# Neighborhood attention on one core: the start regrouped (mark copies, fills, first shifts and PSUM banks moved between engines)

## The chip, the cores and the metric

The kernel runs on 1 core of one Trainium2 chip. The metric is device time in microseconds (us) of one execution; the profile adds one profiled execution with every instruction's engine, start and duration. Engines: PE does matrix products, DVE, ACT and POOL do elementwise work and copies, and SP only issues transfers (DMA). Each engine takes its instructions in order; an engine's queue of DMA issues is named SPq, ACTq or POOLq here. Matrix products land in PSUM, which has eight banks; everything else lies in SBUF, 128 partitions wide.

## The reference

The input is a 224 x 224 image with 192 channels in bf16. Every pixel attends to the 7 x 7 pixels around it with a step of 2, the window clamped at the borders, with one softmax over the 49:

```
qkv = x @ wqkv;  q, k, v = split(qkv)
r0 = clip(ir - 6, 0, H - 13);  ri = r0[:, None] + 2 * arange(7)     # the same for columns
logits = einsum('bnc,bnkc->bnk', q, k[neighbours]) * 192 ** -0.5
p = softmax(logits)
o = einsum('bnk,bnkc->bnc', p, v[neighbours]) @ wo
```

## The kernel before

**Folded weights.** Logits are x_q (Wq Wk^T) x_k, so the kernel forms AW = Wq Wk^T (scaled) once and then G = AW applied to the queries; the keys are x itself. In the same way WP = Wv Wo is formed once, and V = x WP already has the output projection in it.

**Layout.** Because the step is 2, pixels of odd and even rows and columns don't mix; rows are kept in two classes `rc`, columns in two classes `cc`. `load_items(b)` (line 145) brings in one strip `b` of 16 image rows by three transposing DMAs on SP, so that channels lie on partitions: XA[0] and XA[1] hold 128 channels each of the even and the odd pixel of a column pair, and X1[b] the 64 that are left of both. `xb_items` (158) copies the latter into XB[0] and XB[1], 64 partitions each. The other 64 partitions of XB hold marks: rows of numbers that, multiplied with a one-hot row or column of G, add a very negative value to the logits of keys outside of the window. `marks(m, v0, v1, eng)` (227) copies a block of rows of such marks; XB has 48 rows of each class, used as a ring. `sort_items(b, rc, eng)` (167) and `first_sort` (365) copy a strip into XS in the order in which V is computed.

**Steps and pairs.** The work goes in 14 steps `n`: seven tiles `ti` of 16 class rows, for each of the two row classes. A step has 14 column slots `s`, taken two at a time in seven pairs `m`. A pair goes through:

- stage1: logits `s` on PE (line 497), their negated maximum `nmx` on DVE (499)
- stage1b: the exponentials `p` on ACT (507)
- stage2, one pair later: transposes of `p` on PE (517), copied to SBUF by DVE (519)
- stage3, two pairs later: P V on PE (528) with V from VF and VD
- stage4: the reciprocal of the sums (534) and the product (548) on DVE, then the store (554, 567), mostly on SP, a part on POOL through a list `pool_q`, of which four entries are issued in a pair.

**V and its shifts.** `v_item(rc, cb)` (343) computes V of one column slot into a PSUM tile `pv` and has DVE or ACT evacuate it into VF. VD is VF with the two halves of the partitions exchanged, made by DMAs: `vd_low` (350) and `vd_high` (354). For step 0, V of the rows above comes from `v_first` (358), seven products evacuated by ACT, and the first shifts (line 621) write it into the low half of VD[0] by two DMAs of 64 x 7 pieces.

**G.** For each step four groups of column slots are made: `whole(0)`, `whole(1)` and `halves` (437 to 456). A whole goes from PSUM into G by one evacuation; halves go over `gx`, which ACT evacuates and POOL then copies into G (456). The first group of step 0 is put directly, by ACT and DVE. G's own one-hot rows and columns for the marks are filled by `g_col` (248) and `g_row` (258); `g_row_on` (274) copies such rows on to further slots by DMA.

**Interleaving.** While step n runs its pairs, PE also computes V and G for step n + 1. In step 0 these are its own remaining V (list `v0`) and G as well, in the lists `w128` (677) and `w64` (657). The argument given to an item says whether DVE (true) or ACT evacuates it. The PSUM pools are `ps_g` (three banks, for G and V), `ps_o` (two, for P V), `ps_t` (one) and two for the logits.

**Order.** All queues are written out by hand: the order of the statements is the order on each engine, and `in_order` (89) fixes it. Before the loop (lines 593 to 621) stand the fills of G, the third strip's loads, the sorts and copies of strips 0 and 1, the second block of marks (243 and 604), `v_first`, a warming-up of PE (610) and the first group of G.

Of the kernel before, what the change touches and what calls it, by code (L numbers as in the profile page):

```python
# [9 lines left out]
F32 = mybir.dt.float32  # L10
# [16 lines left out]
MM = 16  # L27
BND = 16 * S
C = 192
VP = 2 * C + 2  # L30
# [68 lines left out]
def kernel(  # L99
# [7 lines left out]
    nc = tc.nc  # L107
# [37 lines left out]
    def load_items(b):  # L145

        src = xp[16 * b:16 * b + 16].rearrange("r j c -> (r j) c")
        at = (16 * b) % (2 * RP) * S

        def one(k):  # L150
            if k == 1:
                X1[b] = x1_p.tile([128, BND], BF, name=f"x1_{b}", tag="x1")
            dst = X1[b][:] if k == 1 else XA[k // 2][:, at:at + BND]
            nc.sync.dma_start_transpose(out=dst.unsqueeze(1), in_=src[:, 128 * k:128 * k + 128])

        return [lambda k=k: one(k) for k in ((0, 2, 1) if b in (0, 2, 3) else (1, 0, 2))]
# [70 lines left out]
    def marks(m, v0, v1, eng):  # L227

        p = 64 - XDAT[m]
        if v0 == 0:  # L230
            eng(out=_win(XB[m], p, 64, S, [[RW, MM], [1, S]]), in_=_win(XB[m], p, 64, 0, [[RW, MM], [1, S]]))
        else:
            eng(out=_win(XB[m], p, 64, v0 * RW, [[1, (v1 - v0) * RW]]), in_=_win(XB[m], p, 64, v0 % MM * RW, [[1, (v1 - v0) * RW]]))
# [6 lines left out]

    for m in range(2):
        marks(m, 0, MM, nc.vector.tensor_copy)
    marks(0, MM, 2 * MM, nc.vector.tensor_copy)

# [1 line left out]
    def g_col(rc, ti, s0, ns, eng):  # L248
        for cc in range(2):
            p = XCOL[cc]  # L250
            if s0 == 0:
                for h in range(2):
                    for (j0, nj) in _runs8(rc, ti, h):
                        eng(out=_win(G[rc][cc], p, 32, NSLOT * 128 + 64 * h + 8 * j0, [[nj, 8], [1, nj]]), in_=_win(CH[cc], p, 32, 0, [[1, 8], [0, nj]]))
            else:
                eng(out=_win(G[rc][cc], p, 32, (NSLOT + s0) * 128, [[128, ns], [8, 16], [1, 8]]), in_=_win(CH[cc], p, 32, 8 * s0, [[8, ns], [0, 16], [1, 8]]))

    def g_row(rc, ti, s0, ns, eng, parts):

        for cc in range(2):  # L260
            p = XROW[cc]
            for (j0, nj, e0, estep) in parts:
                if s0 == 0:
                    for h in range(2):
                        for (r0, nr) in _runs8(rc, ti, h):
                            a, b = max(j0, 8 * h + r0), min(j0 + nj, 8 * h + r0 + nr)
                            if a < b:
                                eng(out=_win(G[rc][cc], p, 32, NSLOT * 128 + 64 * h + 8 * r0 + a - 8 * h - r0, [[nr, 8], [1, b - a]]),
                                    in_=_win(E, p, 32, e0 + estep * (a - j0), [[0, 8], [estep, b - a]]))
                else:  # L270
                    eng(out=_win(G[rc][cc], p, 32, (NSLOT + s0) * 128 + 8 * j0, [[128, ns], [8, nj], [1, 8]]),
                        in_=_win(E, p, 32, e0, [[0, ns], [estep, nj], [0, 8]]))
# [68 lines left out]
                    nc.tensor.matmul(pv[64 * h:64 * h + 64, cc * C:(cc + 1) * C], lhsT=at(k, h), rhs=WP[(cc, pas)][:], start=(pas == 0), stop=(pas == 1))  # L341

    def v_item(rc, cb):
        def emit(dve):
            pv = ps_g.tile([128, 512], F32, name="pv", tag="pg")
            v_mms(pv, lambda k, h: XS[rc][:, k, cb, 64 * h:64 * h + 64])
            evac(_win(VF[rc], 0, 128, cb * VP, [[193, 2], [1, C]]), pv[:, 0:2 * C].rearrange("p (t c) -> p t c", c=C), dve)
        return emit

    def vd_low(rc, c0, c1, eng=nc.sync):  # L350

        eng.dma_start(out=VD[rc][0:64, c0:c1, 0:VP - 1], in_=VF[rc][64:128, c0:c1, 0:VP - 1])
# [240 lines left out]
    g_row(0, 0, 0, 1, pool, first0)  # L593
    g_col(0, 0, 1, 3, pool)
    g_row(0, 0, 1, 3, pool, first0)
    g_col(0, 0, 4, 10, pool)
    g_col(1, 0, 0, 1, pool)
    g_row(1, 0, 0, 1, pool, first1)
    g_row(1, 0, 1, 1, pool, first1)
    for it in load_items(2):  # L600
        it()
    for it in first_sort(dve) + xb_items(0, dve) + xb_items(1, dve) + sort_items(0, 0, dve):
        it()
    marks(1, MM, 2 * MM, dve)
    for j in range(7):
        v_first(j)(False)

# [7 lines left out]
    gw0[0](False)  # L615
    gw0[1](True)
    gh0[0](False, True)
    g_row_on(0, 4, 10)

    for (c0, c1) in ((7, 14), (0, 7)):  # L620
        nc.scalar.dma_start(out=VD[0][0:64, c0:c1, 0:VP - 1], in_=VF[1][0:64, 7:14, 0:VP - 1])
    v0 = [v_item(0, cb) for cb in (13, 0, 1, 2, 3, 4, 5, 6, 7, 8, 9, 10, 11, 12)]
    ld = []

    for k in range(NP + 2):
        J = pairs[k] if k < NP else None
        n = J.n if J else NSTEP
        w64, w128 = [], []
        if J:
            m = J.m  # L630
            if m == 0 and n + 1 < NSTEP:
                rc1 = steps[n + 1][1]
                gw, gh = g_all(n + 1)
                vs = [v_item(rc1, cb) for cb in range(NSLOT)]
            if n == 0:
                w128 = (v0[:9] + gw0[2:4], v0[9:] + gw0[4:6], gw0[6:8] + vs[0:3], gw[0:2] + vs[3:6], gw[2:4] + vs[6:9], gw[4:6] + vs[9:12], gw[6:8] + vs[12:])[m]
                w64 = (gh0 + gh)[m + 1:m + 2]
            elif n + 1 < NSTEP:
                w128 = gw[m + (m > 1):m + 1 + (m > 0)] + vs[2 * m:2 * m + 2]
                w64 = gh[m // 2:m // 2 + 1] if m % 2 == 0 else []  # L640
            stage1(J, 0)
            stage1(J, 1)
            stage1b(J, 0)
            if m == 0 and n + 3 < NBAND:
                ld = load_items(n + 3)
        if k == NP:
            stage2(pairs[k - 1])
        if k >= 2:
            stage3(pairs[k - 2], 0)
            stage3(pairs[k - 2], 1)  # L650
            if k >= NP:
                stage4a(pairs[k - 2], 0)
                stage4a(pairs[k - 2], 1)
            stage4(pairs[k - 2], 0)
            if k == NP - 1:
                stage4a(pairs[k - 2], 1)
        for it in w64:
            it(False)
        if J:
            stage1b(J, 1)  # L660
        if 1 <= k < NP:
            stage2(pairs[k - 1])
        if k >= 2:
            stage4(pairs[k - 2], 1)
        if not J:
            continue

        if m == 1 and 0 < n and n + 1 < NSTEP:
            vd_low(rc1, 9 if n == 1 else 7, 14)
        if n == 0 and m in (4, 6):  # L670
            vd_low(0, *((0, 5) if m == 4 else (5, 9)), nc.scalar)
        if 0 < n and m == 5 and n + 2 < NSTEP:
            vd_low(J.rc, 0, 7)
        if ld:
            ld.pop(0)()
        for i, it in enumerate(w128):
            it(n == 0 and i % (2 if m < 3 else 3) == 1)
            if n == 0 and it is v0[6]:
                vd_high(0, 13, 14)
                vd_high(0, 0, 6)  # L680
            if n == 0 and it is v0[13]:
                vd_high(0, 6, 13)
            if it is vs[6]:
                vd_high(rc1, 0, 7)
            if it is vs[13]:
                vd_high(rc1, 7, 14)
        if n == 0 and m == 0:
            for q in range(2):
                marks(q, 2 * MM, 2 * MM + 3, pool)
        if n == 0 and m == 1:  # L690
            first_vd()
            g_row_on(1, 2, 12)
            g_col_on()
            for it in xb_items(2, dve):
                it()
        if n == 0 and m >= 3:
            marks_on(m % 2, 2 * MM + 3 + (m - 3) // 2)
        add = []
        if n == 0:
            add = {0: sort_items(1, 1, pool), 1: sort_items(2, 1, pool), 3: sort_items(2, 0, pool), 5: xb_items(3, pool) + sort_items(3, 0, pool)}.get(m, [])  # L700
        else:
            if m == 0 and n + 2 < NBAND:
                add = sort_items(n + 2, J.rc, pool)

            if m in (2, 4) and n + 3 < NBAND:
                srt = sort_items(n + 3, J.rc, pool)
                one, two = xb_items(n + 3, pool) + srt[2:], srt[:2]
                add = (two if m == 4 else one) if n > 1 else one + two if m == 4 else []
        pool_q[:0] = add
        if n == 1 and m == 1:  # L710
            g_col(0, 1, 0, 1, pool)
            g_row(0, 1, 0, 1, pool, ((0, 16, MM - 6, 1),))
            g_row(0, 1, 1, 13, pool, ((0, 6, MM - 6, 1),))
        if n == 12 and m == 1:
            last = ((0, 9, 0, 1), (9, 7, 9, 0))
            g_col(1, 6, 0, 1, pool)
            g_row(1, 6, 0, 1, pool, last)
            g_row(1, 6, 1, 13, pool, last[1:])
        pool_do(4 if n + 1 < NSTEP else 3)
# [34 lines left out]
```

## Time and profile before

| What | us |
| --- | --- |
| median of 3 runs (lowest to highest) | 363.57 (362.75 to 363.65) |
| the profiled execution: its time | 363.5 |
| its span | 361.7 |
| busy: PE | 333.8 (92%) |
| DVE | 314.1 (87%) |
| ACT | 307.8 (85%) |
| POOL | 284.4 (79%) |

The busy shares are means over the whole span. In the first three slices of the page, 9 us each, PE is busy for 4, 7 and 7 tenths, ACT for 6, 4 and 4, DVE for 8, 9 and 5 and POOL for 8, 9 and 6; from the eighth slice on PE shows 9 in most. A line of the chain or of the timeline reads: start, length, engine, line of the kernel, what is written from what, number of instructions, and in brackets the idle time before it and what ended it. A group reads: line, engine, operation, count, then busy time in us and mean length of one in ns, then idle time. An engine's length of a DMA issue is the time that its queue was held, not that of the transfer.

### The profile page before, as it was taken

How to read it: one execution, taken by the hardware profiler on the slowest of the kernel's cores; microseconds unless marked ns; L12 is line 12 of the kernel's file. 1: busy time of each engine (PE TensorE's matmuls, PEld its weight loads, DVE VectorE, ACT ScalarE, POOL GpSimd, SP SyncE). 2: the span in 40 equal slices, each digit the busy share in tenths (PEclk: the TensorE clock that was granted, in tenths of full speed). 3: DMA queues.
4: the chain of work that ended last, by engine and by line, in shares of the span. 5: the costliest groups of instructions: out<-in, count | busy, mean ns of one | idle time of the engine just before them, and what ended most of it. 6: DMA issues, size and time to landing. Idle time of an engine off the chain costs nothing.

```text
span 361.7 us, 19481 instructions
## 1 busy us (share of the span) xinstructions
PE 333.8 (92%) x8120; PEld 307.4 (85%) x8120; DVE 314.1 (87%) x743; ACT 307.8 (85%) x824; POOL 284.4 (79%) x450
## 2 busy tenths in 40 slices
PE   4778888998999999999999999999999999999881
PEld 2667777997999999999989999998999999999671
DVE  8956987897898998989989899898998889989992
ACT  6445676897999999989999999998999989999792
POOL 8966699999896996959969699695995868374094
PEclk9989999999999999999999999999999999999998
DMA  9999886699979979889798997988989965634432
GB/s 189 208 184 166 176 167 159 153 178 180 208 155 208 195 166 175 192 192 197 169 188 188 178 193 179 181 202 179 194 186 187 176 144 122 141 96 110 105 78 77
DMA packets 137746, 60.79 MB, mean 168 GB/s; under 512 B 88809, under 2 KB 137134, under 8 KB 137659
## 3 DMA queue, kind: packets, MB, share of 16 engines
q1 hardware_dynamic: 130133, 56.37, 78.7%
q0 software_dynamic: 5520, 1.73, 2.7%
q10 hardware_dynamic: 2006, 1.47, 2.1%
q8 instruction: 63, 1.03, 1.2%
q14 instruction: 24, 0.20, 0.2%
HBM read 0.29 MB, written 19.27 MB: 54 GB/s over the span
## 4 chain that ended last, share of the span: by engine, by line
PE 71%; POOL 10%; DVE 9%; ACT 4%; DMA 2%; issue 2%; POOLq 0%; SPq 0%; DVEq 0%; ACTq 0%
PE pv L341 17%; PE s L497 15%; PE o_ps L528 14%; PE pg L421 10%; PE pt_ps L517 9%; PE pgh L421 5%; POOL out_dram L567 4%; ACT p L507 3%; POOL xs L170 2%; DVE xb L160 2%; POOL out_dram L554 2%; DMA vd<-vf 1%; DVE nmx L499 1%; POOL xb L160 1%; POOL g L456 1%
## 5 line engine op out<-in xcount | busy, mean ns | idle before, releaser
L507 ACT ACTIVATE p<-s,nmx 128x224 bf16<-128x224 f32 x392 | 149.7, 449 | 26.7 <-DVE nmx L499 24.9
L499 DVE TENSOR_REDUCE nmx<-s 128x2 f32<-128x392 f32 (+1 forms) x196 | 102.5, 565 | 19.1 <-PE s L497 17.8
L456 POOL COPY g<-gx 64x512 bf16<-64x512 bf16 (+1 forms) x110 | 61.8, 562 | 56.1 <-ACT gx L331 49.0
L548 DVE TENSOR_TENSOR o_sb<-o_ps,rs 128x384 bf16<-128x384 f32 x179 | 99.8, 557 | 6.2
L341 PE MATMUL pv<-wp,xs 128*64 128x192 bf16 x1624 | 93.2, 251 | 11.4 <-DVE xs L366 3.5
L341 PEld LDWEIGHTS <-xs 128*64 128x64 bf16 x1624 | 79.4, 112 | 24.7 <-issue 9.3
L331 ACT CAST vf<-pv 128x384 bf16<-128x384 f32 x193 | 87.4, 520 | 12.4 <-PE pv L341 11.7
L567 POOL DMA_DIRECT2D out_dram<-o_s x150 | 84.2, 568 | 1.1 <-issue 1.1
L497 PE MATMUL s<-xa,g 128*64 128x196 bf16 (+6 forms) x990 | 82.7, 233 | 2.0 <-DVE g L329 1.1
L528 PE MATMUL o_ps<-vd,pt_sb 128*64 128x193 bf16 x784 | 81.8, 246 | 2.4 <-ACT pt_sb L519 2.1
L497 PE MATMUL s<-xb,g 128*64 128x196 bf16 (+6 forms) x990 | 82.2, 232 | 0.6 <-DVE g L329 0.4
L528 PE MATMUL o_ps<-vf,pt_sb 128*64 128x193 bf16 x784 | 81.9, 247 | 0.1
L497 PEld LDWEIGHTS <-g 128*64 128x64 bf16 x1980 | 78.0, 110 | 4.5 <-issue 2.0
L528 PEld LDWEIGHTS <-pt_sb 128*64 128x64 bf16 x1568 | 71.5, 109 | 4.0 <-ACT pt_sb L519 3.1
L519 DVE COPY pt_sb<-pt_ps 128x1024 bf16<-128x1024 bf16 x93 | 63.7, 686 | 6.1 <-PE pt_ps L517 1.1
L517 PE MATMUL pt_ps<-ident,p 128*64 128x128 bf16 x1568 | 64.2, 219 | 0.0
L517 PEld LDWEIGHTS <-p 128*64 128x64 bf16 x1568 | 57.5, 110 | 5.0
L331 ACT CAST g<-pg 128x512 bf16<-128x512 f32 (+4 forms) x136 | 57.6, 468 | 2.2 <-PE pg L421 2.0
L421 PEld LDWEIGHTS <-aw 128*64 128x64 bf16 x1320 | 55.1, 110 | 3.8 <-issue 0.8
L421 PE MATMUL pg<-xb,aw 128*64 128x512 bf16 (+9 forms) x440 | 54.5, 269 | 0.1
L421 PE MATMUL pg<-xa,aw 128*64 128x512 bf16 (+9 forms) x440 | 52.5, 270 | 0.3 <-DMA xa<-in_x_dram 0.3
L170 POOL COPY xs<-xa 128x896 bf16<-128x896 bf16 x50 | 45.1, 928 | 1.4
(68 smaller groups left out, 277.7 us busy)
## 6 DMA issues: line engine op xcount, KB each, us to landing
vd<-vf SPq DMA_DIRECT2D x49, 336.9 KB
out_dram<-o_sb SPq DMA_DIRECT2D x156, 96.0 KB
out_dram<-o_sb SPq DMA_DIRECT2D x26, 78.0 KB
out_dram<-o_s POOLq DMA_DIRECT2D x78, 9.0 KB, 3.8
vd<-vf SPq DMA_DIRECT2D x2, 337.8 KB
vd<-vf ACTq DMA_DIRECT2D x2, 336.9 KB
xa<-in_x_dram SPq DMA_TRANSPOSE x28
out_dram<-o_s POOLq DMA_DIRECT2D x26, 15.0 KB, 3.8
```

What stands on the lines that cost most here:

```text
L331: nc.scalar.copy(out=out_, in_=in_)
L341: nc.tensor.matmul(pv[64 * h:64 * h + 64, cc * C:(cc + 1) * C], lhsT=at(k, h), rhs=WP[(cc, pas)][:], start=(pas == 0), stop=(pas == 1))
L421: nc.tensor.matmul(o, lhsT=l, rhs=r, start=(pas == 0), stop=(pas == 1))
L456: nc.gpsimd.tensor_copy(out=G[rc][cc][p:p + 64, 1, s0:s0 + ns, :], in_=gx[p:p + 64, 0:ns * 128].rearrange("p (s q) -> p s q", q=128))
L497: nc.tensor.matmul(o, lhsT=w, rhs=r, start=(pas == 0), stop=(pas == 1))
L499: nc.vector.tensor_reduce(out=nmx[:], in_=_win(s_ps, 0, 128, lo, [[256, 2], [16, 14], [1, 16 - lo]]), axis=AX.XY, op=ALU.max, negate=True)
L507: nc.scalar.activation(out=J.p[:, ab, cc, :, z:z + 112].rearrange("p q (r k) -> p q r k", k=8), in_=_win(s_ps, 0, 128, cc * 256, [[8, 2], ...
L517: nc.tensor.transpose(pt_ps[64 * h:64 * h + 64, 4 * ab + 2 * cc + q, :], J.p[:, ab, cc, q, 64 * h:64 * h + 64], ident[:])
L519: (nc.scalar.copy if J.n == NSTEP - 1 and J.m < 5 else nc.vector.tensor_copy)(out=J.pt[:], in_=pt_ps[:])
L528: nc.tensor.matmul(o_ps[64 * h:64 * h + 64, cc * 193:cc * 193 + 193], lhsT=J.pt[:, 4 * ab + 2 * cc + q, 64 * h:64 * h + 64], rhs=V[h][:, ( ...
L548: nc.vector.tensor_tensor(out=o_sb[:], in0=_win(o_ps, 0, 128, 0, [[194, 2], [1, C]]), in1=rs[:].unsqueeze(2).to_broadcast([128, 2, C]), op ...
L567: pool_q.append(lambda dst=dst, p=p, m=n * nj, cc=cc: nc.gpsimd.dma_start(out=dst.rearrange("j i c -> i j c"), in_=o_sb[p:p + m, cc, :]))
```

## The change

It touches the start and step 0 only; the computation is the same.

- The second block of marks (rows 16 to 31) is copied by POOL for both XB tiles: the first after the first shifts and a sort, the second at the end of pair 0. Before, DVE did both, at lines 243 and 604.
- The fills `g_col(0, 0, 4, 10)`, `g_col(1, 0, 0, 1)` and `g_row(1, 0, 0, 1)` go from POOL to ACT.
- `g_row_on(0, 4, 10)`, two DMAs on SP, moves ahead of the loads of strip 2.
- The first shifts are issued on POOL's queue instead of ACT's; the sort of strip 1 for class 1 follows them on POOL, ahead of the loop instead of behind pair 0.
- In pairs 0 and 1, four and two of the V products use `ps_o`'s banks, and DVE evacuates six of 11 items and four of seven, where it evacuated five and three.
- The two low shifts of pairs 4 and 6 go from ACT's queue to SP's.
- In step 0 a load of a later strip is issued behind the items of `w128` and their shifts, not ahead of them.

```diff
-    marks(0, MM, 2 * MM, nc.vector.tensor_copy)
...
     def v_item(rc, cb):
-        def emit(dve):
-            pv = ps_g.tile([128, 512], F32, name="pv", tag="pg")
+        def emit(dve, spare=False):
+            pv = ps_o.tile([128, 512], F32, name="pv", tag="o") if spare else ps_g.tile([128, 512], F32, name="pv", tag="pg")
...
-    g_col(0, 0, 4, 10, pool)
-    g_col(1, 0, 0, 1, pool)
-    g_row(1, 0, 0, 1, pool, first1)
     g_row(1, 0, 1, 1, pool, first1)
+    g_col(0, 0, 4, 10, act)
+    g_col(1, 0, 0, 1, act)
+    g_row(1, 0, 0, 1, act, first1)
+    g_row_on(0, 4, 10)
     for it in load_items(2):
         it()
     for it in first_sort(dve) + xb_items(0, dve) + xb_items(1, dve) + sort_items(0, 0, dve):
         it()
-    marks(1, MM, 2 * MM, dve)
...
     gh0[0](False, True)
-    g_row_on(0, 4, 10)
 
     for (c0, c1) in ((7, 14), (0, 7)):
-        nc.scalar.dma_start(out=VD[0][0:64, c0:c1, 0:VP - 1], in_=VF[1][0:64, 7:14, 0:VP - 1])
+        nc.gpsimd.dma_start(out=VD[0][0:64, c0:c1, 0:VP - 1], in_=VF[1][0:64, 7:14, 0:VP - 1])
+    for it in sort_items(1, 1, pool):
+        it()
+    marks(0, MM, 2 * MM, pool)
...
         if n == 0 and m in (4, 6):
-            vd_low(0, *((0, 5) if m == 4 else (5, 9)), nc.scalar)
+            vd_low(0, *((0, 5) if m == 4 else (5, 9)))
...
-        if ld:
+        if ld and n > 0:
             ld.pop(0)()
         for i, it in enumerate(w128):
-            it(n == 0 and i % (2 if m < 3 else 3) == 1)
+
+            if n == 0 and m < 2:
+                it(*(((i in (0, 1, 3, 5, 7, 10), i in (2, 3, 7, 8)), (i % 2 == 0, i in (2, 3)))[m][:2 if it in v0 else 1]))
+            else:
+                it(n == 0 and i % (2 if m < 3 else 3) == 1)
...
+        if ld and n == 0:
+            ld.pop(0)()
         if n == 0 and m == 0:
             for q in range(2):
                 marks(q, 2 * MM, 2 * MM + 3, pool)
+            marks(1, MM, 2 * MM, pool)
...
-            add = {0: sort_items(1, 1, pool), 1: sort_items(2, 1, pool), 3: sort_items(2, 0, pool), 5: xb_items(3, pool) + sort_items(3, 0, pool)}.get(m, [])
+            add = {1: sort_items(2, 1, pool), 3: sort_items(2, 0, pool), 5: xb_items(3, pool) + sort_items(3, 0, pool)}.get(m, [])
```

## The prediction

> **What bounds the kernel now.** I read four views: the page, then the chain of waits over the first 95 us, then the timeline of each engine up to 62 us, then the groups of POOL by shape. The page gives PE 71% of the whole chain, so after the start it is PE's stream that sets the end, and a saving made early is kept if nothing between holds it back. The chain shows who owns the start:
>
> ```profile
> 9.09 1.28 DVE xb L233
> ...
> 12.42 1.58 DVE xb L160
> 14.00 0.03 issue
> 14.03 1.56 DVE xb L160
> ...
> 17.33 1.04 DVE xb L233
> ...
> 84.02 2.69 POOL xs L170 x3
> ```
>
> From 3.9 to 20.4 us the chain is one unbroken run of DVE copies; two are the mark copies of line 233 that the change takes away. Later, from 60.7 to 86.7 us, it is POOL without a gap, and then PE. The timeline shows the gaps:
>
> ```profile
> 11.98 3.13 POOL L256 COPY g<-ch 32x1280 bf16<-32x1280 bf16 x2
> ...
> 12.47 0.48 ACT L331 CAST vf<-pv 128x384 bf16<-128x384 f32 x1 [4.19 <-PE pv L341]
> ...
> 16.67 0.22 PE L421 MATMUL pg<-xa,aw 128*64 128x39 bf16 x2 [0.28 <-DMA xa<-in_x_dram]
> ...
> 19.92 0.65 DVE L329 CAST g<-pgh 64x24 bf16<-64x24 f32 x4
> ...
> 22.93 1.27 POOL L456 COPY g<-gx 64x512 bf16<-64x512 bf16 x2 [3.06 <-issue]
> ...
> 23.88 1.56 PE L341 MATMUL pv<-wp,xs 128*64 128x192 bf16 x24 [0.66 <-DVE vf L329]
> ...
> 24.36 4.66 SPq L154 DMA_TRANSPOSE xa<-in_x_dram  x1
> ...
> 29.12 1.31 SPq L355 DMA_DIRECT2D vd<-vf  x2
> ```
>
> ACT stands idle 4.19 us before 12.47. PE waits for the last transposed strip at 16.67, which no engine work can bring forward; the trace's completion events give 10.18, 12.43, 14.77 and 16.63 us for the third to sixth transposes. DVE's last G evacuation ends at 20.57. In pair 0 the V products wait for bank evacuations. The two windows between the steps of the granted clock:
>
> ```profile
> 18.00:21.29 3.29, 1.89 (x42) 1.52 (x42) 2.92 (x13) 0.48 (x4) 1.73 (x5) 1.00 1.17 184
> 21.29:24.71 3.42, 2.76 (x33) 2.44 (x30) 1.26 (x3) 2.32 (x6) 1.72 (x3) 0.50 1.22 205
> ```
>
> (stretch; PE, weight loads, DVE, ACT, POOL busy; granted clock; DMA.) Prices of POOL:
>
> ```profile
> L567 POOL DMA_DIRECT2D out_dram<-o_s x150 | 84.2, 568 | 1.1 <-issue 1.1
> ...
> L160 POOL COPY xb<-x 64x1792 bf16<-64x1792 bf16 x22 | 36.9, 1676 | 1.1
> ...
> L233 POOL COPY xb<-xb 64x672 bf16<-64x672 bf16 x2 | 1.5, 742 | 0.1
> ```
>
> **The change, part by part.**
>
> *DVE's lead.* Both 64x3584 mark copies leave DVE (1.28 and 1.04 us). DVE is then ready for the first sort at 9.07, but its third copy needs the strip that lands at 10.18: 10.2 to 10.7, where it now ends at 11.68. The two copies of line 160 of 1.58 and 1.56 us lie exactly beside POOL's 32x1280 fills; the fourth, beside smaller fills, takes 0.62. With the big fills on ACT I take 0.65 for each of the four: they end near 13.8 (the second pair waits for 12.43). Sort of strip 0 to 14.8, of strip 1 to 15.6, its last copy at 16.65 to 17.05 after the landing. PE's G products keep their 16.67 start and end at 18.05; DVE follows with 0.65 us of puts and ends at 18.7 where it ended at 20.57. Gain 1.9 at most, 1.0 if POOL now slows the last sort as it slowed line 160. I take **1.6**, nearer the upper end because only three short copies can be hit.
>
> *Fills on ACT.* Small copies on ACT come 0.12 us apart (line 254), a 96x384 copy 0.37 (line 311), so 0.78 ns an element: two of 1280 elements 2.2 to 2.4 us, eight small ones 1.0 to 1.9. Sum 3.2 to 4.3 from 8.29, end 11.5 to 12.6. The first V evacuation could start at 11.5, so it waits 0 to 1.1 us; seven evacuations at 0.43 end by 14.5 to 15.6 against 16.09 now, still ahead of the 16.63 landing. Cost nothing; with that cover gone, up to 1.1.
>
> *POOL's queue.* It loses 7.1 us of fills (3.13 + 1.93 + 2.00). It gains two issues of the first shifts, which wait for the last V evacuation (about 15.2), and two mark copies: from 672 and 1792 elements, 0.84 ns each more, so 3.2 each. In order: shifts 15.2 to 16.3 at 0.57; sort of strip 1 (3 x 0.93) to 19.3 (28.3 now, with no reader before pair 2); marks to 22.5; then line 456, whose first copy is wanted by pair 1's logits and whose input is ready at 21.2: 22.5 to 23.8; small marks (1.5) to 25.3; second marks to 28.5; line 456 to 29.8; next sort to 32.8, where it ends at 35.9 now. Everything behind the new waits still comes before its reader (25.3 us, below). No row shows POOL issuing 448 elements: 0.55 to 0.59 for 6 to 40 elements is flat, which gives 0.57; growing with elements from 40 it would be 6.4. I take 0.57, as the row has no slope, and keep 6.4 for the range.
>
> *SP's queue.* The two row copies of G (2.58) now stand before the three transposes of strip 2, which slip by as much: from 23.55 for the last to at most 29.4 (by then the same bytes had landed before). Their first readers are POOL's sort at 29.8 and DVE's copy near 31: covered, barely. The load of strip 3 (4.66) moves behind the high shifts, which now land at 31.5 and 33.35; without that load's 2.1 us of transfer I expect 31.2. Their reader, pair 0's P V, starts at 34.89 and would start at 31.2, just in time. The two later low shifts (0.60 each) go from ACT's queue to SP's, in a stretch where SP waits for DVE and POOL: nothing for the end, 1.2 us if SP were full.
>
> *Pair 0 and 1 banks.* Nine V products and two G products take PE from 21.3 to 28.3. Five banks instead of three and DVE taking the first two remove the waits of 0.66 and 0.32 us and the wait for ACT behind its exponentials. PE alone needs, at the slow clock of now, 4 x 0.64 + 5 x 0.34 + 0.94 = 5.2 us, so **1.8** less. DVE has six of these (3.5 us), ACT five (2.5): both fit. By the granted clock of 1.0 throughout it would be 9 x 0.34 + 0.94 = 4.0, 1.2 less again. Pair 1 gains the wait of 0.54 us for ACT, but DVE takes one more (0.69 less 0.23 of idle) ahead of the strip copy that holds the next maximum: **0.3**.
>
> The Trainium skill, "TensorE: Matmul & The Clock Gate", Part 1, says that the clock is set by a free-running window of about 3.4 us, half rate after an idle one. The 0.50 row agrees in its 3.42 us, though the window before it was 57% busy, not idle; by that rule the new lead, with shorter gaps, may keep the full clock and the sum would be 1.2 us better, or a window falling elsewhere may cost about that in the lead.
>
> Sum: 1.6 + 1.8 + 0.3 = 3.7 us by the maximum of pair 2 (36.44 now). After it, all is the same work in the same order; POOL reaches pair 2 at 32.8 with its input at about 34.6, so POOL's full stretch starts earlier by the same, and PE behind it. The profiled execution took 363.5, its span 361.7; the median of the runs is 363.57, so no correction: 363.5 - 3.7 = **359.8**.
>
> **The rivals.**
>
> *The transfers take the gain.* The page's DMA row reads 9 in its first four slices, to 36 us. If the shifts on POOL's queue mix into strip 2's transposes, the high shifts land at 33.3 as now, and P V of pair 0 (34.89) gains 1.5 at most: 362.0. For it: the first shifts took 11 us from issue to landing (18.04 to 29.05). Against: one load fewer is ahead.
>
> *POOL's queue runs late, and the kernel is slower.* Line 456's first copy ends at 22.5 + 0.6 = 23.1, and at 23.1 + 2(p - 0.57) with a price p per shift issue. Pair 1's logits start at 28.71 now; from p = 3.4 on the change loses. At p = 6.4 it ends at 34.8: 363.5 + 6.1 - 0.3 = 369.3. For it: no row shows such an issue; against: the flat row. A DVE copy beside it would hold it back as line 160 was held; DVE copies 1.2 us there, so that mechanism alone adds 1.2 (24.3) and hides before 25.3. The Trainium skill, "SBUF — State Buffer", section "SBUF: two separate sides", gives 3.1 us for such an issue beside DVE's copies; by that figure the copy would end at 28.2 and an estimate of the total be 362.7; no run here shows it.
>
> *No change.* The start's gain is given back before 87 us, because POOL and DMA run full there: 363.5. Against: POOL's run starts from a wait for ACT (2.43 us at 38.36), which moves along.
>
> **How the numbers follow.** A difference under 0.3% (1.1 us) can't be told from none. Forecast 0.55 (358.6 to 361.2 by its terms: the clock 1.2 below, lead and banks 1.4 above); transfers 0.18 (361.2 to 362.4); no change 0.10 (to 364.6); slower 0.17. Eight in ten need the first two, and the near half of no change: 358.6 to 363.6. Faster 0.55 + 0.18 = 0.73, same 0.10, slower 0.17.
>
> **What would show it.** DVE's last G put at about 18.7; the line 160 copies at 0.65; ACT's fills over by 12.6; the two shift issues on POOL near 0.57 each, and line 456 at about 22.5; pair 1's first logits near 25.3; PE released by POOL's sort at about 83 instead of 86.7. Wrong would be: POOL issues of several us, PE waiting for POOL in pair 1, or for vd in pair 2.

## The result, and the profile after

The changed kernel takes 366.5 us (median of 12 runs, 364.08 to 369.74), the kernel before 363.61 in as many runs beside it (362.56 to 365.26): a ratio of 1.008, 95% interval 1.0053 to 1.0107, so 2.9 us slower. The forecast was 359.8. Ratios and intervals, here and below, are taken over runs in the fast state alone, the medians beside them over all runs, so the two can differ a little. The profiled execution of the changed kernel, at 364.08 with a span of 362.3, is the shortest of its runs; so its trace shows how the gain goes, and not all of what a usual run loses.

Most line numbers are one or two less than before: logits 496, maxima 498, P V 527, high shifts 354, low shifts 351, first shifts 619, stores 553.

The whole chain by engine, of the page of the changed kernel:

```profile
PE 72%; POOL 7%; DMA 6%; ACT 6%; DVE 5%; issue 2%; POOLq 0%; DVEq 0%; ACTq 0%
```

DVE had 9% and POOL 10% before, DMA 2%: what the change took from DVE and POOL is back as transfers.

The start went as forecast. DVE's timeline of the changed kernel (start, length, engine, line, operation, tiles, count, in brackets the idle time before it):

```profile
10.21 1.45 DVE L160 COPY xb<-x 64x1792 bf16<-64x1792 bf16 x2
11.95 1.32 DVE L160 COPY xb<-x 64x1792 bf16<-64x1792 bf16 x2 [0.29 <-DMA x<-in_x_dram]
...
17.58 0.65 DVE L328 CAST g<-pgh 64x24 bf16<-64x24 f32 x4
...
30.55 1.99 DVE L160 COPY xb<-x 64x1792 bf16<-64x1792 bf16 x2 [0.60 <-DMA x<-in_x_dram]
32.57 1.04 DVE L498 TENSOR_REDUCE nmx<-s 128x2 f32<-128x392 f32 x2
...
62.93 1.04 DVE L498 TENSOR_REDUCE nmx<-s 128x2 f32<-128x392 f32 x2 [0.43 <-PE s L496]
70.95 1.04 DVE L498 TENSOR_REDUCE nmx<-s 128x2 f32<-128x392 f32 x2 [0.17 <-ACT vf L330]
```

The first four strip copies of line 160 take about 0.7 us each, the last G put ends at 18.23 (forecast 18.7), and the maximum of pair 2 starts at 32.57, 3.87 us before the 36.44 of the kernel before (forecast 3.7). The last two rows are pairs 9 and 10, the third and fourth of step 1. The same rows of the kernel before:

```profile
66.98 1.04 DVE L499 TENSOR_REDUCE nmx<-s 128x2 f32<-128x392 f32 x2 [0.42 <-PE s L497]
70.35 1.04 DVE L499 TENSOR_REDUCE nmx<-s 128x2 f32<-128x392 f32 x2 [0.16 <-PE s L497]
```

So at pair 9 the changed kernel is 4.05 us ahead, and one pair later 0.60 behind. All of the gain goes between 62.9 and 71. The chain of waits of the changed kernel over that stretch (start, length, what):

```profile
58.25 0.77 PE pv L340 x13
...
61.61 4.49 DMA vd<-vf
66.10 0.14 issue
66.24 1.50 PE o_ps L527 x16
```

PE's timeline names the wait, the first P V of step 1, and two of the windows show what follows it:

```profile
30.87 0.24 PE L527 MATMUL o_ps<-vd,pt_sb 128*64 128x193 bf16 x1 [0.96 <-DMA vd<-vf]
31.58 0.27 PE L527 MATMUL o_ps<-vd,pt_sb 128*64 128x193 bf16 x1 [0.43 <-DMA vd<-vf]
...
66.24 0.34 PE L527 MATMUL o_ps<-vd,pt_sb 128*64 128x193 bf16 x1 [3.07 <-DMA vd<-vf]
```

```profile
65.78:69.19 3.41, 2.95 (x36) 2.54 (x38) 0.73 (x2) 0.51 (x2) 3.18 (x10) 0.50 0.82 106
```

The columns of a window are the stretch and its length, the busy time of PE, weight loads, DVE, ACT and POOL, the granted clock, DMA share and GB/s. PE waits 3.07 us for one transfer, and the granted clock is then 0.50 for 3.41 us. The 4.65 us lost between pairs 9 and 10 are that wait and some 1.6 us of half clock.

The transfer is the last high shift of step 1's V (`vd_high(rc1, 7, 14)`, slots 7 to 13). The timelines of SP's queue around it, first before, then changed:

```profile
55.87 0.65 SPq L239 DMA_DIRECT2D xb<-xb  x1
56.63 2.66 SPq L554 DMA_DIRECT2D out_dram<-o_sb  x3
59.65 0.66 SPq L355 DMA_DIRECT2D vd<-vf  x1
```

```profile
57.18 0.66 SPq L239 DMA_DIRECT2D xb<-xb  x1
57.94 2.81 SPq L553 DMA_DIRECT2D out_dram<-o_sb  x3
60.86 0.66 SPq L351 DMA_DIRECT2D vd<-vf  x1
61.61 0.64 SPq L354 DMA_DIRECT2D vd<-vf  x1
```

When was its source ready? ACT's evacuations of V, the last of them for step 1 in each kernel, first before, then changed:

```profile
59.14 0.48 ACT L331 CAST vf<-pv 128x384 bf16<-128x384 f32 x1 [0.83 <-PE pv L341]
```

```profile
54.14 0.48 ACT L330 CAST vf<-pv 128x384 bf16<-128x384 f32 x1 [0.23 <-PE pv L340]
```

Before, the data are ready at 59.62 and the issue starts at 59.65. In the changed kernel the data are ready 5.0 us earlier, at 54.62, and the issue comes 2.0 us later, at 61.61. For seven microseconds it stands behind other issues on SP.

For PE it is the landing that counts. By the completion events of the trace the shift lands at 63.72 in the kernel before, and its first reader starts at 67.02 without a wait:

```profile
67.02 0.25 PE L528 MATMUL o_ps<-vd,pt_sb 128*64 128x193 bf16 x1
```

So 3.30 us were to spare. In the changed kernel PE is ready for it at 63.17, 3.85 us earlier, and it lands at 66.10, 2.38 later: less the 3.30 that makes 2.93 of the 3.07 us, and the rest lies between the landing and PE's start.

After pair 10 the changed kernel is between 1.33 us ahead of the kernel before (at pair 15) and 0.62 behind, and the profiled execution ends 0.6 us behind (span 362.3 to 361.7).

### The profile page after: what moved, and what is told of

Read it like the earlier page. It is cut to its first block, busy times and chain, and to the rows that moved or that the text cites. A ratio compares the mean times of both kernels' runs of the same rounds, so it can differ in the third digit from the quotient of the medians.

```text
span 362.3 us, 19483 instructions
## 1 busy us (share of the span) xinstructions
PE 333.3 (92%) x8120; PEld 307.5 (85%) x8120; DVE 311.1 (86%) x743; ACT 310.8 (86%) x832; POOL 287.2 (79%) x444
## 4 chain that ended last, share of the span: by engine, by line
PE 72%; POOL 7%; DMA 6%; ACT 6%; DVE 5%; issue 2%; POOLq 0%; DVEq 0%; ACTq 0%
PE pv L340 16%; PE s L496 15%; PE o_ps L527 15%; PE pg L420 10%; PE pt_ps L516 10%; PE pgh L420 6%; DMA vd<-vf 4%; ACT p L506 4%; DMA x<-in_x_dram 3%; POOL out_dram L566 2%; POOL xs L170 1%; POOL out_dram L553 1%; ACT vf L330 1%; DVE nmx L498 1%; POOL xb L160 1%
## 5 line engine op out<-in xcount | busy, mean ns | idle before, releaser
L340 PE MATMUL pv<-wp,xs 128*64 128x192 bf16 x1624 | 91.6, 249 | 8.0 <-ACT g L330 2.9
L330 ACT CAST vf<-pv 128x384 bf16<-128x384 f32 x191 | 86.3, 521 | 5.9 <-PE pv L340 3.4
L496 PE MATMUL s<-xb,g 128*64 128x196 bf16 (+7 forms) x990 | 82.1, 232 | 1.3 <-POOL g L455 0.8
L170 POOL COPY xs<-xa 128x896 bf16<-128x896 bf16 x50 | 45.9, 944 | 1.4
```

The costliest lines, as they stand in the source:

```text
L330: nc.scalar.copy(out=out_, in_=in_)
L496: nc.tensor.matmul(o, lhsT=w, rhs=r, start=(pas == 0), stop=(pas == 1))
```

## The experiments

The theory after the result (A in the expectations): SP's queue, with the transfers behind it, sets the pace of the first 60 us; the change gives the engines 4 us, but makes the queue later, and the gain becomes PE's wait. Rivals: the two low shifts on SP alone do it; the first shifts on POOL's queue delay what follows (B); POOL's full run, or PE itself, holds the gain back (C); it is the phase of the clock. "Pair 9" and "pair 10" below are the starts of these pairs' first maximum against the profiled execution before.

### One issue or two moved

**e1**: the changed kernel with step 0's low shifts back on ACT's queue.

```diff
-            vd_low(0, *((0, 5) if m == 4 else (5, 9)))
+            vd_low(0, *((0, 5) if m == 4 else (5, 9)), nc.scalar)
```

> The changed kernel, with the two low shifts of pairs 4 and 6 issued on ACT's queue again. Theory A (SP's queue is full up to about 62 us, so the high shift of step 1's last V slots, issued at 61.61 and landed at 66.10, holds PE's first P V of step 1 for 3.07 us): SP is relieved of two issues of 0.67 us, the high shift is issued at about 60.2 and lands near 64.7, PE's wait falls to about 1.6 us, and the time falls by 1.4 to 2 us under the changed kernel's. Rival B (the first shifts on POOL's queue delay strip 2's transposes, and that delay is what is carried on): the low shifts are a small part, the time falls by less than 1 us. Neither expects the whole 4 us of the start.

Measured: 365.33 against 363.9, 1.0049 (1.002 to 1.0078). By the ratios some 1.1 us of the 2.9 are back, short of the 1.4 to 2 expected, and the intervals overlap. The high shift still goes out at 61.46, PE waits 2.31 us for it, the gain falls from 3.64 at pair 9 to a loss of 0.48 at pair 10. Two issues fewer, and in this execution SP is no earlier: other issues took longer (a marks' transfer of line 239 1.58 us instead of 0.63, a store 1.38 instead of 1.05). The low shifts alone don't explain the loss.

**e2**: the changed kernel with the high shift itself on ACT's queue.

```diff
-                vd_high(rc1, 7, 14)
+                vd_high(rc1, 7, 14, nc.scalar if n == 0 else nc.sync)
```

> The changed kernel, with the one high shift at the end of step 0 (step 1's V slots 7 to 13) issued on ACT's queue instead of SP's. Theory A: it is issued when its V is there, near 55 to 56 us, lands by 61 us, PE's first P V of step 1 does not wait, the half clock after 65.8 us is gone, and the 4 us of the start are kept: 359.5 to 360.5 us, and the spread between runs shrinks. Rival B or a further wait behind it: the wait moves to another shift or to POOL's sorts, and the time stays above 362.5.

Measured: 364.92 against 363.9, 1.0027 (1.0001 to 1.0054), where 359.5 to 360.5 was expected. The wait of step 1 is gone; the profiled execution waits elsewhere, at pair 0:

```profile
33.08 0.24 PE L527 MATMUL o_ps<-vd,pt_sb 128*64 128x193 bf16 x1 [1.85 <-DMA vd<-vf]
34.73 0.27 PE L527 MATMUL o_ps<-vd,pt_sb 128*64 128x193 bf16 x1 [1.38 <-DMA vd<-vf]
```

The changed kernel has 0.96 and 0.43 us there. Nothing that e2 edits comes before these waits, so they vary from run to run (this execution was a long one, 368.4 us); after 80 us DVE waits 3.29 and 1.12 us for stores to leave their buffers. By the ratios (1.0080 to 1.0027, intervals that just overlap) to free this one transfer takes back about 1.9 of the 2.9 us, but brings nothing of the engines' gain.

**e3**: the kernel before with its low shifts on SP.

```diff
-            vd_low(0, *((0, 5) if m == 4 else (5, 9)), nc.scalar)
+            vd_low(0, *((0, 5) if m == 4 else (5, 9)))
```

> The kernel before, with only the two low shifts of pairs 4 and 6 moved from ACT's queue to SP's. Theory A: the high shift is issued 1.3 us later (59.65 to about 61.0) and lands near 65.1, but PE's first P V of step 1 starts at 67.0 there, so nothing waits: the same time within 0.3%. If the two issues cost by themselves, 1.3 us slower.

Measured: 365.6 against 363.9, 1.0048 (1.0024 to 1.0071): 1.7 us slower (0.9 to 2.6 by the interval), where no change was expected. The high shift is issued at 60.56 and PE waits 0.79 us for it at 66.52. So these two issues aren't free in the kernel before either.

**e4**: the changed kernel with the first shifts on ACT's queue, for B.

```diff
-        nc.gpsimd.dma_start(out=VD[0][0:64, c0:c1, 0:VP - 1], in_=VF[1][0:64, 7:14, 0:VP - 1])
+        nc.scalar.dma_start(out=VD[0][0:64, c0:c1, 0:VP - 1], in_=VF[1][0:64, 7:14, 0:VP - 1])
```

> The changed kernel, with the first shifts issued on ACT's queue again. Rival B: strip 2's last transpose, landed at 30.5 in the changed kernel, lands at 28 or earlier, SP's queue runs 2 us earlier from there on, PE's wait in step 1 falls from 3.07 to about 1 us, the time falls by 2 us or more. Theory A: the same bytes go through the same transfer engines in the first 40 us, SP reaches its first store at 42 to 43 us as now, the wait stays above 2 us and the time within 1 us of the changed kernel's.

Measured: 367.23 against 363.9, 1.0093 (1.0064 to 1.0121). The high shift is issued at 62.91, PE waits 3.74 us, and two windows follow at half clock:

```profile
66.63:70.04 3.41, 2.51 (x28) 2.09 (x30) 0.73 (x2) 0.06 (x1) 3.23 (x8) 0.50 0.65 128
70.04:73.46 3.42, 3.42 (x45) 2.97 (x43) 1.33 (x3) 2.77 (x6) 2.77 (x6) 0.50 1.21 146
```

SP comes to its first store at 43.76 us, no earlier than in the changed kernel (42.56). POOL's queue is not the cause; B falls.

### Work taken off SP's queue, and a later start

**f1, f2**: the changed kernel and the one before, both without the stores that step 0 issues on SP (that part of the output is not written).

```diff
-                    put(nc.gpsimd if nj < 8 and (s % 2 == 1 if J.n == 0 else s not in (3, 6, 9)) else nc.sync)
+                    if not (J.n == 0 and not (nj < 8 and s % 2 == 1)):
+                        put(nc.gpsimd if nj < 8 and (s % 2 == 1 if J.n == 0 else s not in (3, 6, 9)) else nc.sync)
```

> The changed kernel with the stores of step 0 that go over SP left out (the 18 or so issues of about 0.8 us between 42 and 62 us; those rows of the output are not written). Theory A (the queue of SP and its transfers, never idle to about 100 us, set the pace there, so that engines that start 4 us earlier only wait): the high shift at the end of step 0 is issued when its V is there, near 53 us, PE does not wait in step 1, and the 4 us are kept: 359 to 360.5 us. Rival C (POOL's full run from 44 to 87 us, or PE, holds the gain back): the time stays within 1 us of the same cut in the kernel before.

> The kernel before with the same stores left out. Theory A: with SP relieved the engines are the bound here, which lie 4 us behind those of the changed kernel: 362.5 to 363.5 us, so the changed kernel with the same cut is 3 to 4 us faster. Rival C: this cut alone brings the kernel before as far as the changed one.

Measured: f1 362.55 against 364.33, 0.9954 (0.9917 to 0.9991); f2 363.85, 1.0003 (0.9966 to 1.0041). SP's timeline of f1:

```profile
51.79 0.59 SPq L351 DMA_DIRECT2D vd<-vf  x1
55.27 0.59 SPq L354 DMA_DIRECT2D vd<-vf  x1
```

The source is ready at 55.25 and the high shift goes out at 55.27, with idle time on the queue before it. PE has no wait in step 1: the profiled execution of f1 (361.31) is 3.45 us ahead at pair 9 and at pair 10, 3.46 at pair 35, and 2.8 at pair 91. With room on the queue the gain is kept in this execution. The cut takes away the stores' transfers as well as their issues, so it doesn't tell the queue from what it carries. The same cut gives the kernel before nothing, so PE doesn't wait for the queue there. In medians f1 is 1.3 us faster than f2, with intervals that overlap, in traces 2.3 at pair 9 (3.45 less 1.19); the expected 3 to 4, and the 359 to 360.5 for f1, were too much. As far as this difference holds, C falls.

f2 shows why the traces must be read with care. It is the same as before up to the first store, but has no window at half clock near 21 us; from pair 1 to pair 28 it is 1.2 us ahead of the profiled execution before (0.6 at pair 91). So some 1.2 of the changed kernel's 4 us is the clock's phase in that one execution of the kernel before. The engines' gain at equal clock is 2.3 to 2.9 us.

**f3**: the kernel before with DVE's first mark copy made three times, a later start by 2.3 us.

```diff
     marks(0, MM, 2 * MM, nc.vector.tensor_copy)
+    marks(0, MM, 2 * MM, nc.vector.tensor_copy)
+    marks(0, MM, 2 * MM, nc.vector.tensor_copy)
```

> The kernel before, with the mark copy of DVE's lead (1.28 us) made three times instead of once, so that all of the start is about 2.5 us later and nothing else changes. If the chain through DVE sets the end, as the prediction had it, the time grows by 2.5 us. Theory A: the transfers go on as before, P V of step 1 has 3.3 us of slack to its shift, and the time grows by less than 1 us.

Measured: 366.43 against 364.33, 1.0067 (1.0034 to 1.0101), 2.1 us slower (1.2 to 3.7 by the interval); pair 0 starts 2.34 us later. Under 1 us was expected if the queue alone set the pace. So the queue does not set the pace of the kernel before: its engines do, with the 3.30 us to spare at the high shift that are shown above, and a later start of theirs costs in full. An earlier one is kept only as far as the transfers leave time to spare.

### More shifts on ACT's queue

**e5**: e1 and e2 together. **g2**: e5 with step 0's first two high shifts on ACT's queue too, five in all.

```diff
-            vd_low(0, *((0, 5) if m == 4 else (5, 9)))
+            vd_low(0, *((0, 5) if m == 4 else (5, 9)), nc.scalar)
...
-                vd_high(0, 13, 14)
-                vd_high(0, 0, 6)
+                vd_high(0, 13, 14, nc.scalar)
+                vd_high(0, 0, 6, nc.scalar)
...
-                vd_high(rc1, 7, 14)
+                vd_high(rc1, 7, 14, nc.scalar if n == 0 else nc.sync)
```

> The changed kernel with the two low shifts of step 0 and the last high shift of step 0 on ACT's queue. If it is the number of issues on SP that counts, SP gains 1.3 us on the run with the high shift alone on ACT, and the time falls under the kernel before: 361 to 363 us. If SP and ACT share what makes and carries their transfers, SP is no earlier, and the time stays at that run's 364.9 within 1 us.

> The changed kernel with five shifts of step 0 off SP's queue, on ACT's: both low ones, the last high one, and the two high ones of pair 0, which stand behind the last transpose of strip 2 (held 5.2 us on SP's queue) in the changed kernel. If the order on SP's queue is what makes them late, they land by 29 us, PE's wait of 1.4 us for them in pair 2 goes, with the later waits for half clocks, and the time falls to 361 to 363 us. If the transfers themselves are the limit until 40 us, the strip copy waits longer for its transpose in exchange, and the time stays at 364 to 365.

Measured: e5 364.93 against 364.33, 1.0011 (0.9977 to 1.0044); g2 364.68 against 364.16, 1.0029 (0.9997 to 1.006). Neither has the wait of step 1. Both wait at pair 0's P V instead, e5 1.49 and 1.12 us, g2 1.36 at 32.84, and at 33.07 DVE's strip copy waits 1.62 us for its transpose. They come out level with the kernel before, not faster: another queue for the issue doesn't make the transfers quicker. The Trainium skill, "DMA: Bandwidth & Descriptors", section "SWDGE vs HWDGE vs iDMA", says that transfers from the scalar, sync and gpsimd queues end up on the same 16 DMA engines and interleave; these waits agree.

### The changed kernel again, and its two halves

**g1**: the changed kernel once more, no edit.

> The changed kernel as it is, for a second profile, since the one shown first (364.08 us) was the fastest of its runs. Theory A (SP's queue and its transfers set the pace of the first 100 us): PE waits again for the high shift at the first P V of step 1, followed by one or two windows of half clock, and what makes the run slower than 364.1 are waits for shifts (DMA vd) in this or later steps, not POOL or DVE.

Measured: 365.49, a single execution. The same wait: PE 2.79 us at 66.46 for the shift issued at 61.47, half clock from 67.30 to 70.71, 3.53 us ahead at pair 9 and 1.05 behind at pair 10. The profiled case was no accident.

**g3**: the engines' part alone. All DMA issues are on the queues and in the order of the kernel before; the mark copies, fills, the sort's place, the banks and the choice between DVE and ACT are the change's. **g4**: the queues' part alone, in the kernel before:

```diff
+    g_row_on(0, 4, 10)
     for it in load_items(2):
...
-    g_row_on(0, 4, 10)
...
-        nc.scalar.dma_start(out=VD[0][0:64, c0:c1, 0:VP - 1], in_=VF[1][0:64, 7:14, 0:VP - 1])
+        nc.gpsimd.dma_start(out=VD[0][0:64, c0:c1, 0:VP - 1], in_=VF[1][0:64, 7:14, 0:VP - 1])
...
-            vd_low(0, *((0, 5) if m == 4 else (5, 9)), nc.scalar)
+            vd_low(0, *((0, 5) if m == 4 else (5, 9)))
...
-        if ld:
+        if ld and n > 0:
             ld.pop(0)()
...
+        if ld and n == 0:
+            ld.pop(0)()
```

g3 is this diff turned round, made to the changed kernel.

> The engines' part of the change alone: marks and sort on POOL, fills on ACT, banks and evacuations of pairs 0 and 1; all DMA issues on the queues and in the order of the kernel before. Theory A: SP's queue is then as in the kernel before, the high shift lands near 64 us, PE has 2 to 3 us less slack than it gains, so a part of the start is kept at best: 362 to 364 us, at most 0.3% slower than before. If the engines' part itself is what costs, it is 366 us.

> The queues' part of the change alone, in the kernel before: first shifts on POOL's queue (behind its fills), the row copies of G ahead of strip 2's loads, strip 3's loads behind pair 0's shifts, the two low shifts on SP. Theory A: the engines gain nothing and SP gets two issues more: slower, about as the low shifts alone (365.6), 365 to 367 us. If the queues' part is harmless, 363.5 to 364.5.

Measured: g3 364.7 against 364.16, 0.9993 (0.995 to 1.0036), its runs from 360.09 to 369.37; g4 368.73, 1.0156 (1.0098 to 1.0215), 4.6 us slower by the medians, 5.7 by the ratio. For g3 362 to 364 us was expected, at most 0.3% slower; for g4 365 to 367, which was too little. PE's timeline of g4, and SP's of g3:

```profile
68.87 0.34 PE L528 MATMUL o_ps<-vd,pt_sb 128*64 128x193 bf16 x1 [2.50 <-DMA vd<-vf]
```

```profile
55.05 2.56 SPq L553 DMA_DIRECT2D out_dram<-o_sb  x3
57.71 0.66 SPq L354 DMA_DIRECT2D vd<-vf  x1
```

The engines' part brings the high shift's issue forward from 59.65 to 57.71, by 1.9 us; the queues' part puts it back to 63.85, by 4.2. Together that makes 2.3 later, and the changed kernel has 2.0. In g4 the data are ready at 57.82, six microseconds ahead of the issue, and PE waits 2.50 us in a kernel that is only 0.84 ahead. g3's profiled execution (360.09) has no wait in step 1 (the shift lands at 61.82, and PE wants it at 63.62) and keeps 3.4 us to the end; it is its best run. So the loss comes with the queues' part: alone it costs clearly, and without it there is none. That the engines' part alone is a gain, one execution shows and the median does not.

## Why the prediction was wrong, step by step

**Right in the sum, in part by luck: the engines' terms.** DVE's lead: the forecast 1.6 us came out as 2.3 at pair 0. Of this, the fills of POOL that lay beside DVE's copies were read rightly: without them a strip copy takes 0.73 and 0.66 us instead of 1.58 and 1.56. But in this execution the sixth transpose also landed earlier, at 15.94 instead of 16.63; in six others with the same code up to pair 0 (e1, e2, e5, f1, g1, g2) the lead is 0.8 to 1.7. Fills on ACT end at 12.33 (forecast 11.5 to 12.6) and cost nothing. Lead and banks together, 3.7 forecast by pair 2, measured 3.87. That leaves 1.5 for the banks (3.87 less 2.34) where 2.1 were forecast; by f2, 1.2 of it is the phase of the clock, and only some 0.3 the banks' own (0.6 in g1 and 0.7 in f1, reckoned likewise). The 1.8 for pair 0 had the half clock on both sides; at the full clock, which the changed kernel had, the prediction's own figures give 1.2 more. So the banks were sized 1.4 to 1.8 too high, and an earlier strip and a better clock made up for it.

**Right: POOL's queue.** POOL's timeline of the changed kernel:

```profile
16.08 1.65 POOL L619 DMA_DIRECT2D vd<-vf  x2 [2.66 <-ACT vf L330]
...
20.47 3.17 POOL L233 COPY xb<-xb 64x3584 bf16<-64x3584 bf16 x1
23.70 1.28 POOL L455 COPY g<-gx 64x512 bf16<-64x512 bf16 x2
```

The two issues took 0.92 and 0.74 us, nearer the 0.57 that I took than the far end of 6.4; the mark copy 3.17 (3.2), and line 455 came at 23.70 where 22.5 was forecast, and cost PE at most 0.50 and 0.29 us of waits. The rival with p from 3.4 falls. The Trainium skill, "SBUF — State Buffer", section "SBUF: two separate sides", gives about 3.1 us for a DMA of this queue that overlaps a DVE copy; these two, with only the end of DVE's last sort copy (0.39 us long) and the first G puts beside them, don't show it.

**Wrong: "The two later low shifts … go to SP's, in a stretch where SP waits for DVE and POOL: nothing for the end, 1.2 us if SP were full."** SP was not waiting. In the kernel before its queue has at most 1.2 us of idle time, all gaps between issues together, in each 10 us up to 100; the lengths of its issues and the idle time behind the semaphores were not told apart in my reading. That is the step that failed: moved issues on SP's queue were priced at nothing. The price for a full queue was in the sentence, but I held it to be unlikely. e3 puts the two issues at 1.7 us in the kernel before, e1 at some 1.1 in the changed one.

**Wrong: strip 2's slip as "covered, barely", and the loads moved in step 0.** Here landings were read at the wrong transfers. By the semaphores that the readers wait for, strip 2's last transpose landed at 29.05 before, not at 23.55, and the first shifts at 23.55 and 27.76, 5.5 and 9.0 us after their issues, not 11; the high shifts of pair 0 landed at 33.35 and 34.27, not at 31.5 and 33.35. Slipped by 2.58 from 29.05, the strip comes at 31.6, behind the copy that wants it near 31. In the changed kernel it landed at 30.52, DVE waited 0.60 us for it (the row at 30.55), and pair 1 took 7.08 us from its first maximum to the next pair's, against 6.87, where 0.3 less was forecast.

The queue goes on late from there. To 42 us it is held mostly by transposes. In the changed kernel and in g4 the same queue comes to its first store at 42.56 and 45.05 us; in g3, with the order of before, at 39.97. In these executions the order of before was worth 2.6 us of queue to the change, more than the two low shifts' 1.34; six others with the changed order come to that store between 41.9 and 43.8. Whether the row copies of G or the moved load count for more was not separated; the first shifts on POOL's queue do not (e4).

**Wrong: "After it, all is the same work in the same order".** It is, for the engines. But SP's stores and shifts are the same work as well, on a queue with no room to make up what the moved issues cost it. "PE behind it" thus failed at 63 us, where PE meets a transfer that has its source ready 7 us before its issue. POOL's stretch did start earlier; PE's wait for its sort near 86 us (0.69 and 0.52 before) is gone.

**The rivals.** Nearest was "The transfers take the gain", but its place was pair 0 and its price at most 2.2 us. At pair 0 it holds in small (0.96 and 0.43 us of waits; the shifts landed at 30.7 and 31.5, the forecast was 31.2). The 11 us that spoke for it was the landing of a transpose, as said. What I lacked was a rival in which the gain of the engines meets a full queue later on, and the moved issues make it a loss: g4's price alone, 4.6 us, set against 2.3 to 2.9, gives 1.7 to 2.3 us slower, and 2.8 to 3.4 with the 5.7 of the ratio; 2.9 was measured. Such sums of medians are uncertain by 2 us or more, and by g3 not even the engines' gain is seen in the median.

**The clock.** Waits of PE are followed by half rate: 2.31 and 3.07 us by one window, 3.74 by two. The Trainium skill, "TensorE: Matmul & The Clock Gate", Part 1, has the window's length (3.41 us here) right. An idle window, which it asks for, is not needed: in the 3.41 us before the half rate PE was still busy for 0.80 us in the changed kernel, and for 0.57 (e4) to 1.34 (g4) in the others with such a wait, while e3's wait of 0.79 us was followed by none.

**Open.** Why a usual run of the changed kernel is 2.4 us above its profiled one, and why g3's runs spread from 360 to 369, is not settled. The profiled executions of e2, e4 and e5 show later waits of 1.1 to 3.3 us for shifts and stores, at other places in each; that such waits make the difference is argued, not shown. No kernel here that does the whole work is clearly faster than the one before.

## What to carry to other kernels

Before a gain of the engines is credited, read the queue that feeds them: for each transfer of the stretch behind, compare the time when its source is ready with the time of its issue, and the time when it lands with the time when its reader starts. Here the first two were equal (59.62 and 59.65), and 3.30 us were to spare at the reader; a gain of 3.85 with a landing 2.38 later used that up and became a wait, while the engines' part alone, which brought the issue forward by 1.9, did not (g3). Ask how long a queue is idle before more issues are given to it (two of 0.6 us cost 1.7 in e3), and split a change that moves engine work and issues together in these two halves first.

## What the runs showed of the hardware that was not expected

- Two issues moved from SP's queue to ACT's brought SP's next shift forward by nothing: 61.46 us in e1, 61.61 and 61.47 in two executions of the changed kernel. One of SP's issues at line 239 took 1.58 us instead of 0.63; that ACT's issue beside it is the cause is not shown, as short issues of SP took up to 1.1 us without one too (g1).
- Executions of the same code up to there differ by 1.2 us from pair 1 on, by whether one 3.41 us window at half clock falls into the start (before against e3 and f2).
- A DMA of 64 x 7 pieces took 0.74 to 0.92 us to issue from POOL, and landed 6 and 8 us later.
